# Attention and a two-layer MLP on one core: another order for the first batch and the seam of the layers, with re-timed builds

## The chip, the core and the metric

The kernel runs on one core of a Trainium2 chip. TensorE (PE in the rows) multiplies, VectorE (DVE), ScalarE (ACT) and GpSimd (POOL) do the element-wise work, and SyncE (SP) and ScalarE issue the DMAs. Every engine works through its own instruction stream in order, and waits on semaphores. The metric is the device time of one execution in microseconds, the median of several runs. TensorE's granted clock is 1.00 (2.4 GHz) or 0.50 (1.2 GHz) of full speed at any moment; a row shows the mean over its stretch.

## What is computed

Attention over 4 batches, 8 heads, 576 positions and 64 channels, with a causal window of 128 and a linear bias, and then two feed-forward layers of 512 x 2048 on the 2304 tokens:

```python
rel = pos[:, None] - pos[None, :]
mask = (rel >= 0) & (rel < 128)
scores = np.where(mask, scale * (q @ k.T) - slope * np.abs(rel), -1e9)
attn = np.exp(scores - max); attn = attn / (attn.sum() + 1e-9)
x = (attn @ v)                                  # 2304 tokens x 512
h = x @ w1_in;  x = np.maximum(0.01 * h, h) @ w1_out
h = x @ w2_in;  out = (h / (1 + np.exp(-1.702 * h))) @ w2_out
```

Inputs come as 64-bit floats for the weights and as 32-bit floats for q, k and v. Each 32-bit operand of the two layers is held as a high part and a low part, and a product is three passes (high by high, high by low, low by high).

## The kernel before

**Attention.** The work goes in 32 steps `s`, listed in `steps` (L273): a step is a batch `b`, a group `g` of four heads and a block `i`. For i = 1, 2, 3 it handles two neighbouring 64-row blocks of two head pairs; i = 0 handles the three blocks that are left, with six items for the vector engines in place of four. The function `attention` (L834) emits, for each s, the scores of step s, the products with v of step s - 3 and the transposes of step s - 2 on PE, with the bias and maximum (DVE, L403), the exponentials (ACT, L415), the normalising (POOL, L428), the copies out of PSUM (L442, L489) and the subtraction for the low part (L135) between them. Step s = 0 needs only the first blocks of q and k; i = 2 and 3 need the later blocks too. `load_first` (L340) issues the first loads of q, k, a weight block and v on the SP and ACT queues in the order in which they are written. Eight DMA semaphores go round, so an issue also waits until the eighth DMA ahead of it has landed.

**Weights.** A weight block comes as 64-bit words (`load_w`, 512 KB) and is turned into a high and a low part by `conv_w`: an absolute value and a copy on ACT, five operations on DVE, an addition and a subtraction on POOL, spread over 12 ticks. A tick is a place in the emitted program, three per attention step and one per product group. `wconv` lists the blocks (n, p) in order, p = 0 for the in-weights and p = 1 for the out-weights, `convs` names the steps in which one starts, and `wload` the loads.

**Layer 1.** A round is a chunk `c` of 256 hidden channels and a tile `t` of 384 tokens. `mm1` makes two groups of 12 matmuls per round, `mm2` four groups of 6, and `groups` holds their order. From s = 8 one group runs per attention step as soon as its weights are converted and its tokens are there; the rest run in `layer1` (L738) and at the head of `layer2` (L768).

**Layer 2.** A unit (i, p) multiplies a chunk with a pair of token tiles by seven products (L597, 6 matmuls each) in 13 slots; six of the slots are empty and take an output product `out2` of the unit before (L667, 6 matmuls of 512 columns). The operands x of pair p come from `build_x(p, pace)`: seven copies on ACT (L564) and eleven subtractions on DVE (L135, 128x768), operation d being emitted `int(d * pace)` ticks after the start. The seven hidden results of a unit pass through `gate` (a tanh on ACT, L609, and a multiplication on DVE, L610) and `split` (a copy on ACT, L524, and a subtraction on POOL, L135) before `out2` can use them. `load_out` fetches the out-weights of a unit.

Of the kernel before, what the change touches and what calls it, by code (L numbers as in the profile page):

```python
# [20 lines left out]
CB = 2  # L21
# [10 lines left out]
def attention_mlp_kernel(  # L32
# [24 lines left out]
    def after(d, fn):  # L57
        later.setdefault(step[0] + d, []).append(fn)
# [75 lines left out]
    def sub(e, out, in0, in1):  # L134
        e.tensor_tensor(out=out, in0=in0, in1=in1, op=ALU.subtract)  # L135
# [35 lines left out]
    def conv_w(n, p):  # L171
        early = window[0]
        if early:
            x = 4 * p + n
            af, ops = to_f32(
                n, p, 2, ys[:, 1536:2048].bitcast(U32) if x % 3 == 2 else None,
                ys[:, 2048:2560].bitcast(U32) if x % 2 == 1 else None, (0, 2, 3, 4, 5, 6, 7))
        else:
            af, ops = to_f32(n, p, 4)
        hi, lo = wt[n][:, 2 * p], wt[n][:, 2 * p + 1]  # L180
        run(ops + [
            (10 if early else 7, lambda: nc.scalar.activation(hi, af, AF.Copy)),
            (12 if early else 8, lambda: (
                sub(nc.gpsimd if early else nc.vector, lo, af, hi.bitcast(F32)),
                ready.add((n, p)))),
        ])
# [83 lines left out]

    steps = [(0, g, i) for i in (1, 2, 3, 0) for g in range(2)]  # L273
    steps += [(b, g, i) for b in range(1, B) for g in range(2) for i in (1, 2, 3, 0)]
    NS = len(steps)

# [63 lines left out]
    def load_first(wz):  # L340
        for n in range(2):
            new_qk(n)
        load_q(nc.sync, 0, 0, 0, 4)
        load_q(nc.scalar, 0, 1, 0, 4)
        load_k(0, 0, 4)

        nc.scalar.activation(wz[:, 0:1], wz[:, 1:2], AF.Exp)
        load_k(1, 0, 4)
        load_q(nc.scalar, 1, 0, 0, 4)
        load_q(nc.sync, 1, 1, 0, 4)  # L350
        load_k(0, 4, NKB)
        load_q(nc.sync, 0, 0, 4, NKB)
        load_q(nc.scalar, 0, 1, 4, NKB)
        load_w(*wload.pop())
        load_v_first()
        load_k(1, 4, NKB)
        for a in range(2):
            load_q(nc.sync, 1, a, 4, NKB)
        load_w(*wload.pop())
        load_v(1)  # L360
# [186 lines left out]

    xb = {}  # L550

    def xblocks(extra):
        halves = [xs[:, t, k] for t in (0, 1) for k in range(2)]
# [6 lines left out]
    def build_x(p, pace):  # L560
        b11, b12, b21, b22 = (y1[:, 2 * p + t, 2 * j:2 * j + 2] for j in range(2) for t in range(2))

        def hi(n, src):
            return lambda: nc.scalar.activation(xb[p][n][:, 0], src, AF.Copy)  # L564

        def lo(n, src, e):
            return lambda: sub(e, xb[p][n][:, 1], src, xb[p][n][:, 0].bitcast(F32))

        def diff(out, in0, in1):
            return lambda: sub(nc.vector, out, in0, in1)  # L570


        V = nc.vector
        ops = [
            (0, hi(0, b11)), (1, lo(0, b11, V)), (1, hi(1, b21)), (2, diff(b11, b12, b11)),
            (2, hi(5, b22)), (3, lo(1, b21, V)), (4, lo(5, b22, V)), (5, diff(b12, b22, b12)),
            (6, diff(b22, b22, b11)), (6, hi(3, b12)), (7, hi(2, b22)), (7, lo(2, b22, V)),
            (8, lo(3, b12, V)), (8, hi(4, b11)), (9, diff(b21, b22, b21)), (9, hi(6, b21)),
            (10, lo(4, b11, V)), (11, lo(6, b21, V)),
        ]  # L580
        run([(int(d * pace), fn) for d, fn in ops])
# [9 lines left out]

    def product(i, p, n, out, start, stop):
        w = slots[n]
        x = xb[p][XN[n]]
        ops = [(a, b2, k) for a, b2 in PASS for k in range(2)]
        for m, (a, b2, k) in enumerate(ops):
# [107 lines left out]

    alone = 4
    for j in range(0, alone, 2):
        groups += [(j + c, mm1, f) for c in range(2) for f in range(CB)]
        groups += [(j + c, mm2, e) for c in range(2) for e in range(4)]
    for j in range(alone, NR + 2):
        for ff in range(CB):  # L710
            if j < NR:
# [17 lines left out]
        ch = n // CB - 2  # L729
        return ch < 0 or (pos2 if p else pos1)[0] >= last1[ch] - ahead  # L730

    wconv = [(n, p) for p in range(2) for n in range(2 * CB)]
    wconv += [(n + f, p) for n in range(2 * CB, NF, CB) for p in range(2) for f in range(CB)]
    wload = wconv[:4 * CB]
    wload.reverse()

# [31 lines left out]
    def layer2():  # L768
# [4 lines left out]
        for n in USE:  # L773
            load_in(0, n)

        begun = None
        while groups:
            run_group()
            tick()
            if begun is None and pos2[0] >= NR - 5:  # L780
                begun = step[0]
                build_x(0, 1.5)
        load_out(0)
        assert begun is not None
        after(max(1, begun + 20 - step[0]), lambda: build_x(1, 1.5))
        units = [(c, p) for c in range(NCH) for p in range(2)] + [
            (NCH + c, 2) for c in range(NCH)]
        prev = []
        for k, (i, p) in enumerate(units):
            more = i + 1 < NCH  # L790
            for t, fn in enumerate(unit_ops(i, p)):
# [10 lines left out]
                tick()  # L802
            if p and NCH - 1 <= i < 2 * NCH - 1:
                load_out(i + 1)
            if (i, p) == (NCH - 1, 0):
                after(1, lambda: build_x(2, 1.25))
            prev = [lambda t=t, e=e, i=i, p=p: out2(i, p, t, e) for t in (1, 0) for e in range(3)]
        for _ in range(4):
            tick()
# [19 lines left out]
        for n in range(2 * CB):  # L829
            alloc_w(n)  # L830

    convs = (0, 2, 4, 5, 7, 8, 10, 11)

    def attention():  # L834
        nconv, credit = 0, 0.0
# [124 lines left out]
```

## Time and profile before

| what | value |
|---|---|
| median of 3 runs | 908.07 us (907.67 to 908.46) |
| the profiled execution, its own time | 912.59 us |
| its span | 910.8 us |
| mean granted TensorE clock over the span | 0.982 |
| PE busy | 873.9 us (96%) |
| DVE, ACT, POOL busy | 73%, 47%, 44% |

The span is what the rows cover; 1.79 us of the execution's own time lie around it. The busy share of PE is a mean over stages: the first 80 us, where attention alone runs, differ from the rest, and so do two short stretches near 520 and 765 us. The rows further down are taken from these.

### The profile page before, as it was taken

To read this page: it belongs to the slowest core of one execution; us is meant where nothing else is said; L and a number is where in the kernel's file an instruction comes from. 1 tells how busy PE (TensorE), PEld (TensorE's weight loads), DVE (VectorE), ACT (ScalarE), POOL (GpSimd) and SP (SyncE) were. 2 spreads that over 40 slices of the span, in tenths; PEclk is the share of its full clock that TensorE was granted. 3 is DMA by queue.
4 is the path that set the end of the run, shared out by engine and by line. 5 is a ranking of instruction groups with operands and counts; after the bars stand their busy time and mean duration, and the time that the engine had idled before them with its cause. 6 is when DMAs were issued, how large, how long until landed. Compare 5 with 4: busy or idle time off the path is not lost.

```text
span 910.8 us, 16665 instructions
## 1 busy us (share of the span) xinstructions
PE 873.9 (96%) x6106; PEld 812.6 (89%) x6106; DVE 660.9 (73%) x1337; ACT 427.1 (47%) x1060; POOL 397.9 (44%) x457
## 2 busy tenths in 40 slices
PE   4699999999999999999999989999999998999997
PEld 3577989999999999999999878888888887988896
DVE  4888773688878999899974765777777778344554
ACT  3788885554333444434433455444434344343331
POOL 4697554364445656465662133323333332222221
PEclk7999999999999999999999989999999998999999
DMA  8764432225222342534141242343344327756553
GB/s 211 169 160 105 119 87 72 72 91 170 73 71 70 139 162 70 174 136 162 50 174 70 70 129 100 119 150 110 105 154 153 96 79 200 234 167 207 162 186 70
DMA packets 78626, 116.11 MB, mean 127 GB/s; under 512 B 40912, under 2 KB 41936, under 8 KB 77520
## 3 DMA queue, kind: packets, MB, share of 16 engines
q1 hardware_dynamic: 76784, 114.61, 41.5%
q8 instruction: 49, 0.80, 0.3%
q10 hardware_dynamic: 1760, 0.43, 0.2%
q14 instruction: 33, 0.27, 0.1%
HBM read 87.23 MB, written 27.79 MB: 126 GB/s over the span
## 4 chain that ended last, share of the span: by engine, by line
PE 86%; DVE 5%; issue 3%; DMA 2%; ACT 1%; POOL 1%; SPq 0%; DVEq 0%; POOLq 0%; ACTq 0%
PE mm L667 22%; PE mm L533 11%; PE S L597 10%; PE S L509 10%; PE pt L509 10%; PE O L533 9%; PE pt L597 5%; PE O L597 3%; PE O L469 2%; PE pt L434 2%; PE S L385 2%; PE mm L509 2%; DMA raw<-w1i 1%; DMA y<-v 1%; DVE x L135 1%
## 5 line engine op out<-in xcount | busy, mean ns | idle before, releaser
L135 POOL TENSOR_TENSOR g<-u,g 128x384 fp32r<-128x384 f32 x156 | 171.4, 1103 | 304.8 <-ACT g L524 224.1
L667 PE MATMUL mm<-wB,g 128*128 128x512 f32 x540 | 143.8, 396 | 3.8 <-ACT g L524 2.1
L678 DVE SCALAR_TENSOR_TENSOR y<-mm,y 128x512 f32<-128x512 f32 x126 | 86.9, 689 | 57.8 <-PE mm L667 57.1
L667 PEld LDWEIGHTS mm<-wB,g 128*128 128x128 f32 x540 | 100.8, 189 | 21.8 <-ACT g L524 2.4
L167 POOL TENSOR_TENSOR ca<-ca,cb 128x512 f32<-128x512 f32 x59 | 78.4, 1328 | 52.2 <-DVE cb L165 49.4
L667 PE MATMUL mm<-wB,gm 128*128 128x512 f32 x324 | 87.6, 398 | 3.7 <-POOL gm L135 1.8
L524 ACT ACTIVATE g<-u 128x384 fp32r<-128x384 f32 x156 | 81.3, 522 | 12.8 <-DVE u L610 10.2
L609 ACT ACTIVATE u<-sn 128x384 f32<-128x384 f32 x72 | 37.8, 525 | 91.7 <-DVE sn L625 80.6
L135 POOL TENSOR_TENSOR gm<-u,gm 128x384 fp32r<-128x384 f32 x36 | 36.8, 1036 | 99.0 <-ACT gm L524 65.4
L157 DVE TENSOR_SCALAR ca<-ca 128x512 f32<-128x512 f32 x62 | 46.5, 751 | 45.8 <-ACT ca L156 43.0
L597 PE MATMUL S<-x,wA 128*128 128x384 f32 x384 | 78.9, 341 | 0.0
L597 PEld LDWEIGHTS S<-x,wA 128*128 128x128 f32 x384 | 69.4, 192 | 4.2 <-ACT sn L620 1.3
L667 PEld LDWEIGHTS mm<-wB,gm 128*128 128x128 f32 x324 | 60.5, 190 | 12.6 <-POOL gm L135 2.1
L543 DVE TENSOR_TENSOR y<-y,mm 128x384 f32<-128x384 f32 x88 | 48.2, 548 | 21.2 <-PE mm L533 20.7
L533 PE MATMUL mm<-g,wA 128*128 128x384 f32 x312 | 63.2, 337 | 0.0
L533 PE MATMUL mm<-g,wB 128*128 128x384 f32 x312 | 63.2, 337 | 0.0
L620 ACT ACTIVATE sn<-S 128x384 f32<-128x384 f32 x72 | 34.7, 482 | 55.6 <-PE S L597 55.6
L597 PE MATMUL pt<-x,wA 128*128 128x384 f32 x288 | 58.0, 336 | 0.8 <-DVE sn L625 0.8
L161 DVE SCALAR_TENSOR_TENSOR ca<-raw,ca 128x512 uint32<-128x512 uint32 x62 | 58.5, 944 | 0.2
L165 DVE SCALAR_TENSOR_TENSOR cb<-raw,cb 128x512 f32<-128x512 uint32 x60 | 57.3, 954 | 0.6
L597 PEld LDWEIGHTS pt<-x,wA 128*128 128x128 f32 x288 | 51.4, 188 | 5.4 <-DVE sn L625 1.3
L515 ACT ACTIVATE u<-S 128x384 f32<-128x384 f32 x42 | 20.5, 489 | 74.3 <-PE S L509 69.0
(128 smaller groups left out, 1881.0 us busy)
## 6 DMA issues: line engine op xcount, KB each, us to landing
wA<-w7d SPq DMA_DIRECT2D x112, 256.0 KB, 2.9
w7d<-c SPq DMA_DIRECT2D x8, 1792.0 KB, 6.5
wB<-wod SPq DMA_DIRECT2D x36, 256.0 KB, 4.8
raw<-w1i SPq DMA_DIRECT2D x16, 512.0 KB, 3.7
raw<-w1o SPq DMA_DIRECT2D x16, 512.0 KB, 3.6
raw<-w2o SPq DMA_DIRECT2D x16, 512.0 KB, 4.5
raw<-w2i SPq DMA_DIRECT2D x16, 512.0 KB, 3.5
wod<-wB SPq DMA_DIRECT2D x28, 256.0 KB, 2.9
```

The source lines that it names most:

```text
L135: e.tensor_tensor(out=out, in0=in0, in1=in1, op=ALU.subtract)
L157: lambda: nc.vector.tensor_scalar(af, af, F32_MIN_EXP, F32_MAX_EXP, op0=ALU.max, op1=ALU.min),
L161: lambda: nc.vector.scalar_tensor_tensor(out=a, in0=hi32, scalar=0xC0000000, in1=a, op0=ALU.bitwise_and, op1=ALU.bitwise_or),
L165: lambda: nc.vector.scalar_tensor_tensor(out=bf, in0=lo32, scalar=2.0 ** -52, in1=bf, op0=ALU.mult, op1=ALU.mult),
L167: lambda: nc.gpsimd.tensor_tensor(out=af, in0=af, in1=bf, op=ALU.add),
L509: nc.tensor.matmul(out=h, lhsT=w[:, a, k * 128:(k + 1) * 128], rhs=xs[:, t, b2, k], start=(m == 0), stop=(m == len(ops) - 1),)
L524: nc.scalar.activation(g[:, 0], u, AF.Copy)
L533: nc.tensor.matmul(out=y, lhsT=wt[c * CB + f][:, 2 + a, e * 128:(e + 1) * 128], rhs=gt[r, f][:, b2, :], start=(m == 0), stop=(m == len(ops ...
L543: nc.vector.tensor_tensor(out=acc, in0=acc, in1=y, op=ALU.add)
L597: nc.tensor.matmul(out=out, lhsT=w[:, 256 * a + 128 * k:256 * a + 128 * k + 128], rhs=x[:, b2, k], start=(start and m == 0), stop=(stop an ...
L667: nc.tensor.matmul(out=y, lhsT=gt[i, p, f, t][:, b2, e * 128:(e + 1) * 128], rhs=out_slot(i, f, a), start=(m == 0), stop=(m == len(ops) - 1),)
L678: nc.vector.scalar_tensor_tensor(out=acc, in0=y, scalar=0.5, in1=acc, op0=ALU.mult, op1=ALU.add)
```

## The change

The first batch's steps are written as three of group 0 (i = 1, 2, 3), three of group 1, and then the two with i = 0; they alternated between the groups before. The first loads are put in that order, so the later blocks of q and k of group 0 and the first weight block go ahead of group 1's first blocks. `wconv` now takes both in-blocks of a chunk and then both out-blocks, chunk by chunk, and the eight conversions start in steps 1, 3, 4, 6, 8, 9, 11, 12. In layer 1's first four rounds all groups of chunk 0 on a tile stand ahead of those of chunk 1. The last six groups of layer 1 are left for the six empty slots of layer 2's first unit, the first `load_out` moves behind that unit, and the three builds run at paces 1.8, 1.7 and 1.8 in place of 1.5, 1.5 and 1.25, the second starting 13 ticks after the first (or at once, if these have passed) instead of 20.

```diff
-    steps = [(0, g, i) for i in (1, 2, 3, 0) for g in range(2)]
+    steps = [(0, g, i) for g in range(2) for i in (1, 2, 3)] + [(0, 0, 0), (0, 1, 0)]
...
-        load_k(1, 0, 4)
-        load_q(nc.scalar, 1, 0, 0, 4)
-        load_q(nc.sync, 1, 1, 0, 4)
         load_k(0, 4, NKB)
         load_q(nc.sync, 0, 0, 4, NKB)
         load_q(nc.scalar, 0, 1, 4, NKB)
+        load_q(nc.scalar, 1, 0, 0, 4)
         load_w(*wload.pop())
+        load_k(1, 0, 4)
+        load_q(nc.sync, 1, 1, 0, 4)
...
     for j in range(0, alone, 2):
-        groups += [(j + c, mm1, f) for c in range(2) for f in range(CB)]
-        groups += [(j + c, mm2, e) for c in range(2) for e in range(4)]
+        for c in range(2):
+            groups += [(j + c, mm1, f) for f in range(CB)] + [(j + c, mm2, e) for e in range(4)]
...
-    wconv = [(n, p) for p in range(2) for n in range(2 * CB)]
-    wconv += [(n + f, p) for n in range(2 * CB, NF, CB) for p in range(2) for f in range(CB)]
+    wconv = [(n + f, p) for n in range(0, NF, CB) for p in range(2) for f in range(CB)]
...
-        while groups:
+        while len(groups) > 6:
             run_group()
             tick()
             if begun is None and pos2[0] >= NR - 5:
                 begun = step[0]
-                build_x(0, 1.5)
-        load_out(0)
+                build_x(0, 1.8)
         assert begun is not None
-        after(max(1, begun + 20 - step[0]), lambda: build_x(1, 1.5))
+        after(max(1, begun + 13 - step[0]), lambda: build_x(1, 1.7))
...
-        prev = []
+        prev = [run_group] * len(groups)
...
+            if k == 0:
+                load_out(0)
             if (i, p) == (NCH - 1, 0):
-                after(1, lambda: build_x(2, 1.25))
+                after(1, lambda: build_x(2, 1.8))
...
-    convs = (0, 2, 4, 5, 7, 8, 10, 11)
+    convs = (1, 3, 4, 6, 8, 9, 11, 12)
```

SP's queue at the very start, the two programs against each other (q and k of the first batch, `raw` a weight block, `y<-v` the first v; 256 columns are the first blocks of k, 320 the later ones):

```order
 L297 DMA q<-q 64x4x64 x2
-L303 DMA y<-k 128x2x256 x2
-L297 DMA q<-q 64x4x64 x2
+L303 DMA y<-k 128x2x256
 L303 DMA y<-k 128x2x320
 L297 DMA q<-q 64x5x64 x2
 L127 DMA raw<-w1i 128x1024
+L303 DMA y<-k 128x2x256
+L297 DMA q<-q 64x4x64 x2
 L327 DMA y<-v 128x2x640
 L329 DMA y<-v 64x2x640 x2
```

Group 1's first blocks of k and half of its first q moved behind the first weight block; v and what follows it keep their place.

PE where layer 1 meets layer 2, before (S, O, pt and mm are PSUM tiles; L533 is `mm2`, L597 a product of a unit, L667 `out2`):

```order
L533 MATMUL mm<-g,wB 128x384 x6
L533 MATMUL O<-g,wB 128x384 x6
L597 MATMUL S<-x,wA 128x384 x6
L597 MATMUL O<-x,wA 128x384 x6
L597 MATMUL S<-x,wA 128x384 x6
L597 MATMUL pt<-x,wA 128x384 x6
L597 MATMUL S<-xe,wA 128x384 x12
L597 MATMUL pt<-x,wA 128x384 x6
L597 MATMUL S<-x,wA 128x384 x6
L667 MATMUL mm<-wB,g 128x512 x6
```

and now, from the last group of `layer1`'s order on (the products stand on L599):

```order
L533 MATMUL O<-g,wB 128x384 x6
L599 MATMUL S<-x,wA 128x384 x6
L533 MATMUL mm<-g,wB 128x384 x6
L599 MATMUL O<-x,wA 128x384 x6
L599 MATMUL S<-x,wA 128x384 x6
L533 MATMUL O<-g,wB 128x384 x6
L599 MATMUL pt<-x,wA 128x384 x6
L533 MATMUL mm<-g,wB 128x384 x6
L599 MATMUL S<-xe,wA 128x384 x6
L533 MATMUL O<-g,wB 128x384 x6
L599 MATMUL S<-xe,wA 128x384 x6
L533 MATMUL mm<-g,wB 128x384 x6
```

The first unit's products no longer stand in a row; a group of `mm2` lies in each gap.

DVE from the start of the third build, in unit (7, 1), before (L135 are the build's subtractions, L678 adds up `out2`, L625 and L610 serve the gates):

```order
L135 TENSOR_TENSOR x<-y,x 128x768
L678 SCALAR_TENSOR_TENSOR y<-mm,y 128x512
L135 TENSOR_TENSOR y<-y 128x768
L625 TENSOR_TENSOR sn<-sn,O 128x384
L135 TENSOR_TENSOR x<-y,x 128x768
L610 SCALAR_TENSOR_TENSOR u<-u,sn 128x384
L678 SCALAR_TENSOR_TENSOR y<-mm,y 128x512
L135 TENSOR_TENSOR xe<-y,xe 128x768
L135 TENSOR_TENSOR y<-y 128x768
L678 SCALAR_TENSOR_TENSOR y<-mm,y 128x512
L135 TENSOR_TENSOR y<-y 128x768
L135 TENSOR_TENSOR x<-y,x 128x768
```

and now (L680, L627 and L612 for L678, L625 and L610):

```order
L135 TENSOR_TENSOR x<-y,x 128x768
L680 SCALAR_TENSOR_TENSOR y<-mm,y 128x512
L627 TENSOR_TENSOR sn<-sn,O 128x384
L135 TENSOR_TENSOR y<-y 128x768
L612 SCALAR_TENSOR_TENSOR u<-u,sn 128x384
L680 SCALAR_TENSOR_TENSOR y<-mm,y 128x512
L135 TENSOR_TENSOR x<-y,x 128x768
L680 SCALAR_TENSOR_TENSOR y<-mm,y 128x512
L135 TENSOR_TENSOR xe<-y,xe 128x768
L627 TENSOR_TENSOR sn<-sn,pt 128x384
L680 SCALAR_TENSOR_TENSOR y<-mm,y 128x512
L135 TENSOR_TENSOR y<-y 128x768 x2
```

The subtractions are drawn apart: seven of them stood among these twelve rows, six do now.

## Rows read from the trace of the kernel before

**Rows 1.** The page's head.
```profile
span 910.8 us, 16665 instructions
```

**Rows 2.** Windows: start:end us, length, busy us of each engine, PE clock, DMA.
```profile
42.10:77.50 35.40, 29.28 (x427) 24.50 (x427) 31.38 (x111) 29.61 (x106) 31.43 (x44) 0.95 0.57 142
...
98.10:517.40 419.30, 419.20 (x3078) 414.19 (x3078) 334.85 (x627) 196.90 (x475) 213.64 (x228) 1.00 0.33 108
517.40:534.10 16.70, 11.39 (x44) 9.63 (x44) 14.21 (x18) 8.51 (x16) 5.46 (x4) 0.80 0.09 20
...
763.50:776.30 12.80, 9.15 (x31) 7.77 (x30) 8.68 (x13) 4.12 (x8) 3.67 (x3) 0.73 0.85 226
```

**Rows 3.** Timeline, PE, attention: start us, us, instruction, idle before and releaser.
```profile
21.21 2.15 PE L385 MATMUL mm<-y,q 64*64 64x192 f32 x14 [7.10 <-DMA q<-q]
...
42.08 0.88 PE L385 MATMUL S<-y 64*64 64x192 f32 x16
45.13 1.68 PE L469 MATMUL O<-pt,v 64*64 64x128 f32 x32 [2.17 <-ACT pt L442]
```

**Rows 4.** Chain that ended last, in order of time: start us, us, what.
```profile
16.41 8.29 DMA raw<-w1i
24.72 0.68 ACT ca L156
```

**Rows 5.** Timeline, SP queue, the load of k for batch 1, group 0.
```profile
34.21 0.62 SPq L303 DMA_DIRECT2D y<-k  x1
```

**Rows 6.** The page's DMA issues: count, KB each, median us to landing.
```profile
y<-k SPq DMA_DIRECT2D x6, 576.0 KB, 5.1
```

**Rows 7.** Timeline, PE, where layer 1 meets layer 2.
```profile
516.34 1.21 PE L597 MATMUL pt<-x,wA 128*128 128x384 f32 x6
517.38 1.22 PE L597 MATMUL S<-xe,wA 128*128 128x384 f32 x6
...
525.80 0.50 PE L667 MATMUL mm<-wB,g 128*128 128x512 f32 x1 [2.05 <-ACT g L524]
528.09 2.50 PE L667 MATMUL mm<-wB,g 128*128 128x512 f32 x5 [1.78 <-POOL g L135]
...
534.09 1.55 PE L667 MATMUL mm<-wB,g 128*128 128x512 f32 x6
```

**Rows 8.** Timeline, DVE and POOL, in the same stretch.
```profile
518.96 1.09 POOL L135 TENSOR_TENSOR g<-u,g 128x384 fp32r<-128x384 f32 x1 [10.64 <-ACT g L524]
...
519.11 1.76 DVE L135 TENSOR_TENSOR y<-y 128x768 f32<-128x768 f32 x1
```

**Rows 9.** Timeline, PE, during the third build.
```profile
763.48 1.55 PE L667 MATMUL mm<-wB,g 128*128 128x512 f32 x6
764.87 1.21 PE L597 MATMUL S<-x,wA 128*128 128x384 f32 x6
767.90 0.49 PE L667 MATMUL mm<-wB,gm 128*128 128x512 f32 x1 [1.82 <-ACT gm L524]
770.23 2.50 PE L667 MATMUL mm<-wB,gm 128*128 128x512 f32 x5 [1.84 <-POOL gm L135]
...
776.32 1.54 PE L667 MATMUL mm<-wB,gm 128*128 128x512 f32 x6
```

**Rows 10.** Timeline, DVE and ACT, during the third build.
```profile
764.13 0.54 DVE L610 SCALAR_TENSOR_TENSOR u<-u,S 128x384 f32<-128x384 f32 x1
764.60 0.68 DVE L678 SCALAR_TENSOR_TENSOR y<-mm,y 128x512 f32<-128x512 f32 x1
765.20 0.94 DVE L135 TENSOR_TENSOR y<-y 128x768 f32<-128x768 f32 x1
766.06 0.54 DVE L625 TENSOR_TENSOR sn<-sn,pt 128x384 f32<-128x384 f32 x1
...
766.17 0.84 ACT L564 ACTIVATE x<-y 128x768 fp32r<-128x768 f32 x1 [2.16 <-DVE y L135]
...
766.92 0.92 ACT L524 ACTIVATE gm<-u 128x384 fp32r<-128x384 f32 x2
```

More of the change, by code (lines that the diff above doesn't have):

```diff
@@ L173, in conv_w @@
         if early:
-            x = 4 * p + n
+            x = wconv.index((n, p))
             af, ops = to_f32(
@@ L545, in mm2 @@
         after(1, evac)
-    xb = {}
+    xb, built = {}, set()
     def xblocks(extra):
@@ L566, in lo @@
         def lo(n, src, e):
-            return lambda: sub(e, xb[p][n][:, 1], src, xb[p][n][:, 0].bitcast(F32))
+            return lambda: (sub(e, xb[p][n][:, 1], src, xb[p][n][:, 0].bitcast(F32)),
+                            built.add((p, n)))
         def diff(out, in0, in1):
@@ L593, in product @@
         w = slots[n]
+        assert (p, XN[n]) in built
         x = xb[p][XN[n]]
```

## The prediction

> **What bounds the kernel now.** I first looked at the windows over the whole span. PE never pauses for 419.3 us in the middle [rows 2], and outside three places it is full, so time is PE's own work plus what PE loses at those places: the first 77 us, the seam of the layers (called A, near 520 us) and the third build (B, near 765 us). Anything that PE loses there comes back one for one, since behind each place it is full again and nothing but its own work sets the end.
>
> A: the windows show 11.39 us of work in 16.70, at a clock of 0.80 [rows 2]. In the timeline, neighbouring starts give the undisturbed prices: a product of six 384-column matmuls 1.04 us (516.34 to 517.38, [rows 7]), an `out2` group 1.39 us (763.48 to 764.87, [rows 9]). Between 517.38 and 534.09 stand six products and one `out2`: 6 x 1.04 + 1.39 = 7.63 us. They took 16.71, so A loses **9.08 us**: 16.70 - 11.39 = 5.31 idle, and 3.77 because PE runs slowly after the last two waits (five matmuls in 2.50 us, [rows 7]; 5/6 of 1.39 would be 1.16).
>
> B in the same way: between 763.48 and 776.32 stand two `out2` groups and three products, 2 x 1.39 + 3 x 1.04 = 5.90 us, and 12.84 passed [rows 9]. B loses **6.94 us**, of which 12.80 - 9.15 = 3.65 are idle [rows 2] and the rest is clock.
>
> The start: step 3 waits 7.10 us for its q [rows 3]. From there the steps come every (42.08 - 21.21) / 5 = 4.17 us [rows 3]. Up to 77.5 us no engine is full: PE 29.28, DVE 31.38, ACT 29.61, POOL 31.43 of 35.40 [rows 2]; it is a chain from engine to engine that sets the pace.
>
> **The change, part by part.**
>
> *First steps and loads.* Steps 1 and 2 become those of group 0, whose later q and k now come early; step 3 asks only for group 1's first blocks. The bytes ahead of group 1's last q are the same ones, so that q still lands near 21 to 22 us. The wait stays, but at step 4 instead of 3: **one step more** is behind the kernel when it ends. The chain that follows says whether this is worth something: it goes through the second weight block, landed at 24.72, and ACT's operation on it [rows 4]. That conversion now starts in step 3 instead of 2, so the same block at the same time also stands one step later. Hence one step, 4.17 us. What this collides with: the k of step 8 is issued on SP at 34.21 behind weight loads that wait for conversions [rows 5], none of which gets earlier, and such a load takes 5.1 us [rows 6]: 34.8 + 5.1 = 39.9, where step 8 would like 42.08 - 4.17 = 37.9. PE would wait 2.0 us there; but the next products with v started only at 45.13, after 2.17 us for a copy on ACT [rows 3], and 45.13 - 4.17 = 41.0 is behind 39.9 + 0.9. Only DVE's work of step 8 is late; I charge 0.5, between 0 and 2.
>
> *Order of weights and groups.* From step 8 each step has one group; the first twelve are the same four `mm1` and eight `mm2`, now 2, 4, 2, 4 instead of 4, 8. Two `mm1` leave the stretch up to 77.5 us for the full one after it, where each costs 1.04 more than an `mm2` (12 matmuls against 6): 2.1 us lost. What they free before is one POOL subtraction each (1.09, [rows 8]) and a copy on ACT, on engines at 84 to 89%. I set the balance at -0.4, between -2.5 and +2.
> Start in all: 4.17 - 0.5 - 0.4 = **3.3**, from -0.3 (4.17 - 2 - 2.5) to 6.2.
>
> *Seam A.* The first unit's seven products waited for each other through ACT, DVE and POOL. Six groups of 1.04 us now lie in the gaps. They are moved, not added, so PE's work is unchanged. DVE is the one to check. Prices by neighbouring starts: a build's subtraction 0.86, an addition or gate 0.47, an `out2` sum 0.60 [rows 10]; I price an `mm2` sum as a gate, 0.47. Before, seven products (7.3 us of PE) covered eight subtractions and six small operations, 6.9 + 2.8 = 9.7 us: DVE had to fall behind by 2.4 us, and with POOL's interference by more. Now 13 slots x 1.04 = 13.5 us cover ten subtractions (the second build starts in the first unit's first tick), six sums and six small ones, 8.6 + 2.8 + 2.8 = 14.2 us: nearly level. Two waits should remain. The second product into S waits for ACT's snapshot, behind two build copies (0.84 each, [rows 10]) of which the first waits for a DVE difference: about 0.7. And the first `out2` comes 4 x 1.04 = 4.2 us after the product whose gate it uses, where a later unit has 2 x 1.04 + 2 x 1.39 = 4.9. The chain needs two tanh and two copies on ACT (about 0.9 a pair, as the pair in [rows 10]), two gates on DVE (0.9) and two subtractions on POOL (2.1, [rows 8]), 4.8 of which about 1.0 overlaps; a build's copy (0.84) and DVE's lag where three operations fall in one tick (about 1.3) stand ahead: 5.9 in all, so a wait of about 1.8. Left over 2.5; gain 9.1 - 2.5 = **6.6**, up to 9.1 if both waits close, down to 9.1 - 2.5 - 3.8 = 2.8 if the clock drops as before. `load_out` behind the unit costs nothing: SP reaches it early, and what it overwrites is last read by layer 1's last `mm1`, 13 or more groups ahead of its use.
>
> *Third build B.* At pace 1.25 all eleven subtractions fall in one unit: 11 x 0.86 + 6 x 0.60 + 7 x 0.47 = 16.4 us of DVE beside 7 x 1.04 + 6 x 1.39 = 15.6 us of PE. ACT shows the result: a build copy waits 2.16 us for DVE, and the gates' two copies stand behind it at 766.92 [rows 10]; PE waits for just these [rows 9]. At 1.8 seven of the eleven fall there: 16.4 - 4 x 0.86 = 13.0 of 15.6, and the four others in the next unit, 3.4 + 6.9 = 10.3 of 15.6. The lag goes. The latest block is read one tick or more after its emission, so the slower pace itself adds at most a wait of one subtraction, 0.9; I take 0.2. Gain **6.7**, between 4 and 6.9.
>
> Sum: 3.3 + 6.6 + 6.7 = 16.6 us. The profiled execution took 912.59 (span 910.8, [rows 1]), so 896.0 under the profiler. The median of the runs is 4.5 lower than that execution; the losses are waits and clock in the program itself, so I take them off the median whole: 908.07 - 16.6 = 891.5.
>
> **A rule beside the rows.** A subtraction of the build on DVE took 1.76 us from 519.11 and ended 0.82 after POOL's subtraction had ended at 520.05, as if it had started only then [rows 8]; it is the longest of six among the 33 that ran for 1.3 us or more. The Trainium skill, page "SBUF — State Buffer", section "Who interferes with whom", has a rule that agrees and speaks against packing builds and gates together: a DVE instruction with two SBUF inputs and a GpSimd instruction that reads SBUF exclude each other, and whoever comes first keeps the shared ports for the whole instruction. Taken alone, it would hold four subtractions of the first unit by 0.82 each, 3.3 us more than the 14.2 of DVE, and with these on PE's path the sum would be 13.3 and the time 894.8; my sum has one such meeting in the lag of 1.3.
>
> **The rivals.**
> *Clock at A.* The waits left at A drop the clock again, as it did after 525.80 [rows 7]: gain 2.8 there, 12.8 in all, 895.3. For it: DVE is only level. Against: 2.5 us of waiting are left of 5.3.
> *The start gives nothing.* The k of step 8 and the two moved `mm1` eat the step: start -0.3, 13.0 in all, 895.1. For it: SP's order. Against: 45.13.
> *It doesn't do what it says at B*: ACT's queue and not the pace set the wait, and B keeps its loss: 9.9 in all, 898.2. Against: ACT waited for DVE.
> *Slower.* The builds run beside more gates and sums, and every subtraction meets POOL: 33 x (1.76 - 0.94) = 27.1 us more of DVE [rows 8, 10], all of it shown to PE where DVE is level. It decides above (16.6 + 1.8) / 0.82 = 23 stretched subtractions of 33, and ends at 908.07 - 16.6 + 27.1 = 918.6. Against: six were stretched, and each POOL subtraction can hold one of them only; a unit has four. By the Trainium skill's rule above it is this lock that would decide.
>
> **How the numbers follow.** Forecast 0.72 (gains of 13 to 22), clock at A 0.12, no gain at the start 0.09, B kept 0.03, slower 0.03, and 0.01 for a sum that cancels. The terms' ends make 908.07 - (6.2 + 9.1 + 6.9) = 885.9 and 908.07 - (-0.3 + 2.8 + 4.0) = 901.6; the range 885.5 to 900 leaves out the corner where all three are at their worst. Faster by over 0.2% (1.8 us, about what a measurement of this kernel can tell from no change) 0.96, within 0.01, slower 0.03.
>
> **What would show it.** Right: PE's longest DMA wait stands before step 4 and not 3, and step 8's scores start at 38 to 41 us; in the first unit of layer 2 PE's waits sum to under 3 us at a clock of 1.00; no wait and no lower clock in the third build, with DVE below nine tenths there; PE full otherwise. Wrong: a wait of several us for k at step 8 or for a weight at steps 8 to 16; gates' copies behind build copies on ACT at A; a product of the last pair waiting for its x; build subtractions near 1.7 us in a row.

## The result and the profile after

The changed kernel takes **896.47 us**, median of 4 runs (896.23 to 896.67), where the kernel before took 908.27 in the same comparison (907.67 to 908.75, 4 runs): ratio 0.987, 95% interval 0.9853 to 0.9887. That is 11.8 us less. The forecast was 891.5 in a range of 885.5 to 900: the sign and the range held, the forecast itself was 5 us too low.

The head of the page after, against [rows 1]:

```profile
span 894.4 us, 16658 instructions
...
PE 865.6 (97%) x6106; PEld 807.3 (90%) x6106; DVE 653.5 (73%) x1337; ACT 428.5 (48%) x1060; POOL 406.6 (45%) x457
```

Windows of after (start:end us, length, busy us of each engine, PE clock, DMA), against [rows 2]: attention from the scores of step 10 to those of step 16, the full middle, the seam A from the first product of layer 2 to the second unit's second `out2`, and the third build B.

```profile
48.30:79.68 31.38, 26.23 (x421) 22.44 (x421) 28.30 (x101) 25.54 (x95) 27.65 (x39) 0.95 0.48 126
98.10:502.20 404.10, 404.00 (x2949) 399.42 (x2939) 322.47 (x598) 188.78 (x452) 210.43 (x220) 1.00 0.33 110
502.26:523.67 21.41, 18.73 (x103) 17.68 (x103) 21.36 (x31) 12.57 (x22) 7.70 (x5) 1.00 0.08 23
749.60:763.40 13.80, 13.80 (x70) 12.39 (x69) 11.86 (x18) 7.96 (x14) 3.42 (x4) 1.00 0.80 220
```

B is full at a clock of 1.00. The middle still never pauses. At A PE is idle for 2.68 us in place of 5.31, and DVE is now busy all the time there, 21.36 of 21.41 us.

The stretch of [rows 9], from the last `out2` that reads `g` to the second that reads `gm`, takes 5.91 us now, where it took 12.84:

```profile
753.51 1.55 PE L669 MATMUL mm<-wB,g 128*128 128x512 f32 x6
...
759.42 1.55 PE L669 MATMUL mm<-wB,gm 128*128 128x512 f32 x6
```

PE's timeline of after in the attention part (start us, us, instruction, idle before and what ended it), against [rows 3]; the scores of steps 3, 4, 8 and 10, the first product with v, and the first `mm2`:

```profile
13.08 0.88 PE L385 MATMUL mm<-y,q 64*64 64x192 f32 x16
15.86 0.62 PE L469 MATMUL O<-pt,y 64*64 64x128 f32 x10 [1.90 <-DMA y<-v]
...
19.83 1.23 PE L385 MATMUL S<-y,q 64*64 64x192 f32 x16
...
36.75 0.88 PE L385 MATMUL S<-y 64*64 64x192 f32 x16 [0.99 <-DMA y<-k]
...
48.30 0.88 PE L385 MATMUL S<-y 64*64 64x192 f32 x16
...
53.79 0.44 PE L533 MATMUL mm<-g,wA 128*128 128x384 f32 x1 [2.41 <-POOL g L135]
```

Step 3 no longer waits for its q, and neither does step 4; the longest wait for a load is now the 1.90 us for the first v. Step 8 stands 5.33 us earlier than in [rows 3], step 10 7.15 (55.45 before); part of that is a late load in the trace of before, as the next section shows. A wait is new: the first `mm2` directly follows the `mm1` whose result it reads, and waits 2.41 us for POOL.

PE at A in after, against [rows 7], and POOL and DVE in the same stretch, against the 1.09 of [rows 8]:

```profile
517.36 0.50 PE L669 MATMUL mm<-wB,g 128*128 128x512 f32 x1
520.33 1.42 PE L669 MATMUL mm<-wB,g 128*128 128x512 f32 x5 [2.47 <-POOL g L135]
521.59 1.21 PE L599 MATMUL O<-x,wA 128*128 128x384 f32 x6
522.63 1.20 PE L599 MATMUL S<-x,wA 128*128 128x384 f32 x6
```

```profile
510.30 2.44 POOL L135 TENSOR_TENSOR g<-u,g 128x384 fp32r<-128x384 f32 x1 [7.66 <-ACT g L524]
516.97 3.30 POOL L135 TENSOR_TENSOR g<-u,g 128x384 fp32r<-128x384 f32 x2 [4.24 <-ACT g L524]
```

```profile
510.04 1.82 DVE L135 TENSOR_TENSOR x<-y,x 128x768 fp32r<-128x768 f32 x2
...
512.24 1.31 DVE L135 TENSOR_TENSOR y<-y 128x768 f32<-128x768 f32 x1
```

Of the four waits at A one long one is left, 2.47 us at the first `out2`, and PE ran on at full clock behind it; another of 0.21 stands at 514.08. POOL's subtractions for the gates take 2.44 us, and 3.30 for two (two at the same place took 2.67 before, at 525.36).

### The profile page after: what moved, and what is told of

It reads as the page before. It is cut to its first block, busy times and chain, and to the rows that moved or that the text cites. A ratio compares the mean times of both kernels' runs of the same rounds, so it can differ in the third digit from the quotient of the medians.

```text
span 894.4 us, 16658 instructions
## 1 busy us (share of the span) xinstructions
PE 865.6 (97%) x6106; PEld 807.3 (90%) x6106; DVE 653.5 (73%) x1337; ACT 428.5 (48%) x1060; POOL 406.6 (45%) x457
## 4 chain that ended last, share of the span: by engine, by line
PE 87%; DVE 4%; issue 2%; DMA 2%; POOL 2%; ACT 1%; SPq 0%; ACTq 0%; DVEq 0%; POOLq 0%
PE mm L669 21%; PE mm L533 11%; PE S L599 10%; PE pt L509 10%; PE O L533 10%; PE S L509 10%; PE pt L599 5%; PE O L599 2%; PE O L469 2%; PE pt L434 2%; PE mm L509 2%; PE S L385 2%; DMA q<-q 1%; DMA y<-v 1%; POOL g L135 1%
## 5 line engine op out<-in xcount | busy, mean ns | idle before, releaser
L135 POOL TENSOR_TENSOR g<-u,g 128x384 fp32r<-128x384 f32 x156 | 177.1, 1140 | 298.2 <-ACT g L524 217.8
L680 DVE SCALAR_TENSOR_TENSOR y<-mm,y 128x512 f32<-128x512 f32 x126 | 86.9, 690 | 61.7 <-PE mm L669 61.2
L135 POOL TENSOR_TENSOR gm<-u,gm 128x384 fp32r<-128x384 f32 x36 | 38.4, 1081 | 95.1 <-ACT gm L524 76.1
L599 PE MATMUL S<-x,wA 128*128 128x384 f32 x384 | 77.3, 336 | 0.6 <-ACT sn L622 0.6
L599 PEld LDWEIGHTS S<-x,wA 128*128 128x128 f32 x384 | 67.9, 188 | 4.8 <-ACT sn L622 1.5
L533 PE MATMUL mm<-g,wA 128*128 128x384 f32 x312 | 63.6, 337 | 2.4 <-POOL g L135 2.4
L533 PE MATMUL mm<-g,wB 128*128 128x384 f32 x312 | 63.3, 337 | 0.0
L599 PE MATMUL pt<-x,wA 128*128 128x384 f32 x288 | 58.0, 335 | 0.2 <-DVE sn L627 0.2
L533 PEld LDWEIGHTS mm<-g,wA 128*128 128x128 f32 x312 | 54.5, 188 | 2.7 <-POOL g L135 2.7
L599 PEld LDWEIGHTS pt<-x,wA 128*128 128x128 f32 x288 | 51.4, 188 | 4.7 <-DVE sn L627 0.5
```

Source lines behind the costliest of these rows:

```text
L533: nc.tensor.matmul(out=y, lhsT=wt[c * CB + f][:, 2 + a, e * 128:(e + 1) * 128], rhs=gt[r, f][:, b2, :], start=(m == 0), stop=(m == len(ops ...
L599: nc.tensor.matmul(out=out, lhsT=w[:, 256 * a + 128 * k:256 * a + 128 * k + 128], rhs=x[:, b2, k], start=(start and m == 0), stop=(stop an ...
L680: nc.vector.scalar_tensor_tensor(out=acc, in0=y, scalar=0.5, in1=acc, op0=ALU.mult, op1=ALU.add)
```

## Experiments

Between the two profiled executions lie 16.4 us (910.8 and 894.4), as the forecast said (16.6), and between the medians 11.8. So the first question was what the profiled execution of before, 4.5 us above its own median, had lost more than others, and the second what each part of the change gives alone.

### The kernel before once more

> The kernel before, unchanged, for another profile and more times. Theory 1: the first profiled execution was 4.5 us above its own median because PE lost more than usual at A and B (longer waits there and a longer time at the low clock). Then a new profiled execution near 908 us shows A (517.38 to 534.09 in the first trace, 16.71 us, 9.08 lost) and B (763.48 to 776.32, 12.84 us, 6.94 lost) with a sum of losses near 11.5 us in place of 16.0, and the attention part as it was. Theory 2: the 4.5 us lie outside A and B, so a profile near 908 us has A and B with 16 us lost again and is shorter elsewhere, and the parts of the change give less together than one by one.

Median 910.67 (908.68 to 912.66, 12 runs), the other runs of before in this comparison 910.29 (908.28 to 913.15, 19 runs). One execution of this kernel is thus a draw from some 5 us. The new profile (span 908.9) shows A and B as in [rows 7, 9]: the same four waits, 20.99 us from the first product to the second unit's second `out2` (20.87 in the first trace). **Theory 1 falls.** The difference lies at the start: here step 3 begins at 19.44 (21.21 in [rows 3]) and step 20 at 95.54 (98.08).

PE's timeline of this execution at step 3:

```profile
19.44 1.84 PE L385 MATMUL mm<-y,q 64*64 64x192 f32 x16 [6.70 <-DMA q<-q]
20.77 1.80 PE L469 MATMUL O<-pt,y 64*64 64x128 f32 x32
22.50 1.12 PE L434 MATMUL pt<-ident,st 128*128 128x128 f32 x6
23.54 0.72 PE L385 MATMUL S<-y,q 64*64 64x192 f32 x12
```

The first loads land at different times from execution to execution. In the five executions with the old start this wait was 7.10, 6.70, 5.01, 4.76 and 6.85 us, and step 20 began at 98.08, 95.54, 95.86, 95.96 and 97.34 (the last of these lost 1.0 us between steps 10 and 16, and not at the loads).

### The three parts alone

The start alone (steps, loads, `wconv`, `convs`, `groups` as in the diff ahead of the prediction, nothing else):

> Only the order of the first steps, the loads, the weight conversions and the groups of chunk 0 and 1; seam and builds as before. Both theories: the start gains 4.73 us in the traces (from 98.08 to 93.35 at the scores of step 20), and nothing at A or B depends on it, so 908.1 - 4.7 = 903.4 us. A rival of mine from the prediction (the start gives nothing): 908.

908.59 us (906.08 to 910.0), ratio 0.9977 (0.9962 to 0.9991): 2.1 us by the ratio, with 0.8 and 3.5 as the ends. The 4.73 read from the first two traces was too much, since half of it was the late q of one execution.

The seam alone:

```diff
-        while groups:
+        while len(groups) > 6:
...
-                build_x(0, 1.5)
-        load_out(0)
+                build_x(0, 1.8)
...
-        after(max(1, begun + 20 - step[0]), lambda: build_x(1, 1.5))
+        after(max(1, begun + 13 - step[0]), lambda: build_x(1, 1.7))
...
-        prev = []
+        prev = [run_group] * len(groups)
...
+            if k == 0:
+                load_out(0)
```

> Only the seam of the layers: the last six groups of layer 1 fill the empty slots of the first unit, paces 1.8 and 1.7, second build after 13 ticks, the first out-weights loaded behind the unit; start and third build as before. Theory 1: the seam gains 5.7 us against the profiled execution, but less against the timed runs: 1.5 to 4 us, 904 to 906.5. Theory 2: 5.7 us, 902.4.

906.13 us (904.38 to 907.61), ratio 0.9949 (0.9934 to 0.9964): 4.6 us, with 3.3 and 6.0 as the ends, between the two theories.

The third build alone:

```diff
-                after(1, lambda: build_x(2, 1.25))
+                after(1, lambda: build_x(2, 1.8))
```

> Only the third build at pace 1.8 in place of 1.25. Theory 1: 6.5 us against the profiled execution, less against the timed runs: 3 to 5 us, 903 to 905, so that start, seam and third build alone sum to the 11.8 us of the whole change. Theory 2: 6.5 us, 901.5, and the three sum to 16 to 17, more than the whole.

904.02 us (903.83 to 905.07), ratio 0.9928 (0.9915 to 0.9942): 6.5 us, as theory 2 had it. PE's waits of this kernel from 700 us to the end (total us, times, longest) are a single one:

```profile
PE S L597 <- DVE xe L135: 0.2, 1, 0.2
```

The three sum to 13.2 us, each within about 1.4. The whole change on another chip:

> The changed kernel itself beside the kernel before on this chip. By the traces so far, before in its second profile against after: the start 2.2 us (95.54 to 93.35 at step 20's scores), the seam 4.7 (step 20's scores to the fourth output product of the second unit, 443.44 to 438.51, less the clock), the third build and the rest 7: 14 in all, so 896 to 897 where before takes 910.3. If the ratio of 0.987 holds here too, 898.5, and the three parts overlap somewhere.

897.96 us (896.79 to 899.51) against 909.73 (908.22 to 911.33), ratio 0.9873 (0.9857 to 0.989): 11.6 us, with 10.0 and 13.0 as the ends. The intervals of the sum and of the whole overlap; that the parts take something from each other is not shown.

The traces show where. In us: the start of the scores of steps 10 and 20, the time between steps 10 and 16, from step 20 to the second unit's fifth `out2` (A's end; the expectation above counts it as the fourth, without the divided first), and from there to the `out2` of [rows 9] at 776.32 (B's end):

| kernel | step 10 | 10 to 16 | step 20 | 20 to A's end | A's end to B's end |
|---|---|---|---|---|---|
| before, first trace | 55.45 | 29.23 | 98.08 | 443.31 | 234.93 |
| before again | 52.92 | 29.22 | 95.54 | 443.44 | 235.16 |
| third build alone | 53.32 | 29.24 | 95.96 | 443.11 | 228.34 |
| seam alone | 53.17 | 29.29 | 95.86 | 439.76 | 234.07 |
| start alone | 49.27 | 31.11 | 94.04 | 443.11 | 233.99 |
| after | 48.30 | 31.38 | 93.35 | 438.51 | 227.56 |
| full change again | 48.18 | 31.34 | 93.19 | 439.25 | 227.92 |
| paces without fillers (next section) | 53.70 | 30.24 | 97.34 | 442.13 | 233.97 |

The means that follow are of the first seven rows. The B column falls by 6.6 (means of the old and the new pace, 234.54 and 227.94). The A column falls by 4.1 (443.24 to 439.17), and after's first execution was the best of the three. At step 10 the new start is 4.6 us ahead (means 53.14 and 48.58, the late first row left out), gives 2.0 of it back by step 16 (29.25 and 31.28), and is 2.3 ahead at step 20 (95.79 and 93.53). These means sum to 2.3 + 4.1 + 6.6 = 13.0 us. The six steps are not the same in every execution: one with the old start, the last row, took 30.24 us for them, and the other executions of the new start, with its copies as they are, 31.04 to 31.72.

### Fillers or paces at the seam

The kernel before with the paces and the 13 ticks of the seam, without the fillers:

```diff
-                build_x(0, 1.5)
+                build_x(0, 1.8)
...
-        after(max(1, begun + 20 - step[0]), lambda: build_x(1, 1.5))
+        after(max(1, begun + 13 - step[0]), lambda: build_x(1, 1.7))
```

> The kernel before with the two builds of the seam at paces 1.8 and 1.7 (13 ticks) and no fillers in the first unit. Theory: the gain at the seam comes from the six mm2 groups in the gaps; without them more subtractions fall in a first unit that has only seven products as cover, so the four waits there stay or grow: 0 to 3 us slower than before. Rival: the paces bring a part of the 4.6 us of the seam alone.

909.09 us (907.62 to 912.09) against 909.4, ratio 0.9995 (0.9985 to 1.0005): no change. PE's first `out2` in its timeline waits twice as before, only in other shares:

```profile
523.95 0.51 PE L667 MATMUL mm<-wB,g 128*128 128x512 f32 x1 [0.93 <-ACT g L524]
526.65 2.13 PE L667 MATMUL mm<-wB,g 128*128 128x512 f32 x5 [2.19 <-POOL g L135]
```

So the paces alone bring no gain that can be measured in the median (the ends are -0.5 and 1.4 us; in the trace A is 1.1 us shorter, 442.13 against 443.24 in the mean), and the seam needs the six groups in the gaps. The groups with the old paces were not run, so whether the paces add something to them is not shown.

### Why the start gives 2 us back

The changed kernel with the old order of weights and groups, and the changed kernel without a group in step 10:

```diff
-        for c in range(2):
-            groups += [(j + c, mm1, f) for f in range(CB)] + [(j + c, mm2, e) for e in range(4)]
+        groups += [(j + c, mm1, f) for c in range(2) for f in range(CB)]
+        groups += [(j + c, mm2, e) for c in range(2) for e in range(4)]
...
-    wconv = [(n + f, p) for n in range(0, NF, CB) for p in range(2) for f in range(CB)]
+    wconv = [(n, p) for p in range(2) for n in range(2 * CB)]
+    wconv += [(n + f, p) for n in range(2 * CB, NF, CB) for p in range(2) for f in range(CB)]
```

> The changed kernel with the old order of weights and groups (both chunks' in-weights and mm1 first), new steps, loads and conversion times. Theory 3: the step gained at the start (3.7 to 4.0 us at step 10's scores) is spent between steps 10 and 20 (45.05 us in after against 42.62 in before) by the mm2 that directly follows its mm1 (2.41 us of waiting for POOL) and the slow clock behind it. Then steps 10 to 20 take 43 to 43.7 and the kernel is 0.5 to 1.5 us faster than the full change (one group is moved to the full stretch, 1.04 us). Theory 4: the eight conversions, which end one step later in both, set the end of the start, whatever the groups: within 0.5 us of the full change, or slower by the group moved.

```diff
-            credit += 1
+            credit += int(s != 10)
```

> The changed kernel with no group in step 10, so that the first mm2 runs one step later. Theory 3: the wait of 2.41 us and the slow clock behind it go, one group of 1.04 us moves to the full stretch: 0.5 to 1.5 us faster than the full change. Theory 4: 0 to 1 us slower.

With the old groups 897.91 us (897.06 to 898.84), ratio 0.9868 (0.9855 to 0.9881), the same as the full change beside it, though no `mm2` waits for POOL at the start any more: steps 10 to 16 take 31.04 us, against 31.34, and steps 10 to 20 44.71, where theory 3 wanted 43 to 43.7. Without the group in step 10, 901.05 (899.13 to 902.55), 3.1 slower. **Theory 3 falls**: the wait of 2.41 us is idle time that PE has anyway. Without the group, PE waits about as long for DVE at the next scores:

```profile
53.48 1.74 PE L385 MATMUL S<-y 64*64 64x64 f32 x24 [2.56 <-DVE sm L403]
```

From step 16 on PE is full, and there the skipped slot costs: step 16 begins at 80.25 against 79.52, step 20 at 95.54 against 93.19, the first product of layer 2 at 505.79 against 502.12. An `mm1` of 2.08 us left the free stretch for the full one, and a group of 1.04 the steps ahead of step 20.

The next suspect is DVE. Windows up to step 10 and from 10 to 16, of before again and of the full change (DVE is the third engine):

```profile
0.00:52.92 52.92, 35.61 (x498) 27.67 (x498) 38.91 (x159) 34.52 (x128) 34.31 (x65) 0.90 0.75 187
52.92:82.14 29.22, 25.26 (x422) 21.45 (x421) 25.23 (x98) 25.04 (x92) 26.18 (x40) 1.00 0.61 128
```

```profile
0.00:48.18 48.18, 38.67 (x499) 29.38 (x499) 35.94 (x156) 35.01 (x128) 33.11 (x63) 0.82 0.87 207
48.18:79.52 31.34, 26.21 (x421) 22.19 (x420) 28.03 (x101) 25.41 (x95) 27.66 (x39) 0.95 0.48 126
```

DVE does 64.1 us up to step 16 in one (38.91 + 25.23) and 64.0 in the other (35.94 + 28.03). Ahead of step 10 the changed kernel starts its conversions in steps 1, 3, 4, 6, 8 and 9, the kernel before in 0, 2, 4, 5, 7 and 8, and each is spread over 12 ticks (a step has four of them in the listing, and a group one more; the text on the kernel before says three). Of the conversions' operations on DVE, 28 ran ahead of step 10 in the kernel before and 23 in the changed one: 3.0 us of DVE's work are left behind (38.91 - 35.94), and DVE works them off between steps 10 and 16, where it is busy for 28.03 of 31.34 us. POOL is nearly as busy there, 27.66 us.

To test it, the second copy of the transposes in steps 13 to 16 went from DVE to ACT:

```diff
-                att_evac(s - 2, 1, nc.scalar if s < 13 else nc.vector)
+                att_evac(s - 2, 1, nc.scalar if s < 17 else nc.vector)
```

> The changed kernel with the second copy of the transposes in steps 13 to 16 on ACT in place of DVE: four copies of about 0.5 us leave DVE. Theory 4 (DVE, busy 28.03 of 31.34 us between the scores of steps 10 and 16, sets how long these six steps take): 1 to 2 us less there and in the kernel. Rival: the chain from engine to engine sets it, or ACT (25.41 of 31.34) becomes late: no change or slower by up to 1.

896.32 us (894.78 to 898.88) against 909.4, ratio 0.9855 (0.9839 to 0.9871). The window from step 10 to 16:

```profile
48.86:78.59 29.73, 25.49 (x422) 22.10 (x421) 25.56 (x98) 25.76 (x95) 27.98 (x39) 0.94 0.50 132
```

DVE has 2.47 us less to do and the six steps take 1.61 us less, while POOL does as much as before in the shorter time (27.98 of 29.73), so POOL does not set it. DVE is not full either, 25.56 of 29.73: whether its sum of work or its place in the chain from engine to engine holds the steps, this run does not separate. The medians of this kernel and of the full change differ by as much (1.64), but they are from two comparisons, and their intervals overlap. The same edit also stands in a pair within one comparison (below), with 1.9, and there the six steps take 29.75 us in place of 31.44. By its ratio this was the fastest of all kernels run.

### What is left at the seam

The changed kernel with the first build earlier and the second later:

```diff
-                build_x(0, 1.8)
+                build_x(0, 1.5)
...
-        after(max(1, begun + 13 - step[0]), lambda: build_x(1, 1.7))
+        after(max(1, begun + 19 - step[0]), lambda: build_x(1, 1.25))
```

> The changed kernel with the first build at pace 1.5 and the second 19 ticks after it at pace 1.25, in place of 1.8, and 13 ticks at 1.7: fewer of the builds' subtractions in the first unit of layer 2, where nine start now (503.69 to 514.26) and DVE is busy all the time, and more of them ahead of it and behind it, where it is not. Theory 5: the wait of 2.47 us for POOL at the first out2 comes from DVE: POOL's subtractions for the gates take 2.44 and 3.30 for two there in place of 1.0 each, since DVE's subtractions stand in their way, and DVE's own gates are late. Then the wait falls below 1.5 us, POOL's subtractions are shorter, and the kernel is 1 to 3 us faster than the full change (897.96 with before at 909.73: ratio 0.984 to 0.986). Rival: the distance from the first gates to the first out2 is too short whatever DVE does: wait 2 us or more, same as the full change (0.987).

899.96 us (899.14 to 902.46), ratio 0.9898 (0.9883 to 0.9912): slower than the full change by 2 us, where 1 to 3 us faster was expected. (With the edit of the copies on both sides, in one comparison, it is 1.7: 898.06 below against 896.32.) Yet a part of the expected mechanism is there. POOL and PE in the timeline of this kernel:

```profile
516.62 2.72 POOL L135 TENSOR_TENSOR g<-u,g 128x384 fp32r<-128x384 f32 x2 [6.18 <-ACT g L524]
...
519.39 1.43 PE L669 MATMUL mm<-wB,g 128*128 128x512 f32 x5 [1.70 <-POOL g L135]
...
531.88 1.35 PE L599 MATMUL S<-x,wA 128*128 128x384 f32 x6 [2.70 <-ACT sn L622]
```

The wait at the first `out2` fell from 2.47 to 1.70, not below the 1.5 expected, and POOL's two subtractions from 3.30 to 2.72, near the 2.67 of the kernel before. But a wait of 2.70 us stands in the next unit instead, where after had 0.61 and the full change again none. ACT and POOL just ahead of it:

```profile
529.52 1.26 POOL L167 TENSOR_TENSOR ca<-ca,cb 128x512 f32<-128x512 f32 x1
...
530.82 0.63 ACT L217 ACTIVATE wB<-ca 128x512 fp32r<-128x512 f32 x1 [1.85 <-POOL ca L167]
531.35 0.47 ACT L622 ACTIVATE sn<-S 128x384 f32<-128x384 f32 x1
```

A conversion of out-weights and the later build's subtractions share DVE in that unit. A gate among them ran at 527.38 on DVE, where after has it at 525.39, so POOL's subtraction for it (528.56, 1.00 us) came just ahead of the conversion's addition and not well before it. The addition ended at 530.78, and the snapshot of S stands in ACT's queue behind the copy that waits for it: it starts at 531.35 (530.17 in after), while PE comes to this place 0.91 us earlier than in after. DVE's work was moved from one place where PE feels it to another.

The two edits together:

> The two edits together on the changed kernel: later builds, and the copies of steps 13 to 16 on ACT. They lie 400 us apart with PE full between them, so the gains add: 2 to 5 us faster than the full change if both theories hold.

898.06 us (897.52 to 899.39), ratio 0.9874 (0.9862 to 0.9887): 1.9 less than the later builds alone, on the same chip and in the same comparison. The gain at the start and the loss at the seam add. Against the full change (0.9873) nothing is gained, since the later builds bring a loss; 2 to 5 us were expected.

One more run had every output product one slot later, with seven groups of layer 1 left over:

```diff
-        while len(groups) > 6:
+        while len(groups) > 7:
...
-            prev = [lambda t=t, e=e, i=i, p=p: out2(i, p, t, e) for t in (1, 0) for e in range(3)]
+            prev = prev + [lambda t=t, e=e, i=i, p=p: out2(i, p, t, e) for t in (1, 0) for e in range(3)]
```

> The changed kernel with seven groups of layer 1 left over for the units instead of six, so that every output product runs one slot (1.04 us or more) later. If the first out2's wait for POOL at the seam (2.47 us at 520.33) is only a matter of the distance from the gate, it falls to 1.4 or less there and the kernel gains 1 to 2.5 us on the full change. If DVE, full there (5.00 of 5.00 in 510 to 520), sets the pace of the first unit, the wait stays or moves to the next product: no gain.

937.47 us, ratio 1.031. In this kernel the last output product of a unit reads the out-weights of the next one, so it computes something else, and PE waits for their loads (total us, times, longest):

```profile
PE mm L669 <- DMA wB<-wod: 23.9, 15, 5.1
```

At the first `out2` there is no wait in it, so the distance from the gates counts; but two products ahead of it now wait 0.79 us for DVE and 0.64 for ACT, and one behind it 3.12 for ACT. As a whole it says nothing on the time of the full change.

## Why the prediction was right, and where it was wrong

**What bounds the kernel** held: the long middle stayed as it was. From step 20 to the first product of layer 2 pass 415.14 us before, and 408.93 + 6 x 1.04 = 415.17 in the full change, with its six groups moved.

**The start** came to 3.3 in the forecast, 2.1 in the runs of the start alone and 2.3 in the means of the traces. Two terms of it were wrong and cancelled in part. The step gained was priced 4.17 - 0.5 = 3.7; step 10 came 4.6 us earlier. The wait for group 1's q did not move to step 4: that step starts at 19.83 without a wait for a load. The 21 to 22 us for this q came from one late execution; in the four others with the old start it was there by 19.4 to 20.0. For the same reason step 8, at 36.75, came ahead of the 38 to 41 that were named as a sign. The k of step 8 cost PE 0.99 us in after, nothing in the full change again and 2.34 with the old groups, where the text saw a wait of 2.0 and charged 0.5.

The balance of -0.4 for the moved groups should have been -2.3, and by another mechanism: not the `mm1`, whose place makes no difference that can be measured, but the work of the conversions that DVE had left when step 10 came earlier. (That DVE's work holds steps 10 to 16 is shown by the moved copies; no run moved the conversions alone, so their share is argued from the windows.) "The same block at the same time also stands one step later" saw the block's landing and not the DVE work behind it. [rows 2] showed DVE at 31.38 of 35.40 up to 77.5 us; that was the place to ask what the steps that come earlier would have to carry.

**Seam A** is the term that was mis-sized most: 6.6 forecast, 4.1 in the traces, 4.6 for the seam alone. The total of the waits in the first unit was right (2.68 in place of the 2.5), their places were not: 2.47 stand at the first `out2`, where 1.8 were expected, and a second product into S that waits for ACT's snapshot comes only in the next unit (0.61 in after, up to 0.33 in the five below).

What failed is the step from waits to time: the 2.5 us of waiting were taken for all that is left over. From the first product of layer 2 to the second unit's second `out2` stand ten products, six groups and one `out2`, 16 x 1.04 + 1.39 = 18.03 us. After took 21.41, so it lost 3.38: 2.68 idle, and 0.70 in matmuls that ran longer around the two stops. Five other executions with the fillers (the seam alone, the full change again, the old groups, the skipped group, the copies moved to ACT) took 22.96 to 22.99 and lost 4.9 to 5.0: with the same wait of 2.46 or 2.47 us, but with a granted clock of 0.82 or 0.83 over some ten us around and behind it, where after had 1.00. That is the rival that was given 0.12 (gain 2.8). DVE, called nearly level with 14.2 us of work for 13.5, was busy for 21.36 of 21.41 us, and POOL's two subtractions for the first `out2` took 3.30 us in place of the 2.1 priced. PE in the full change again:

```profile
520.18 1.50 PE L667 MATMUL mm<-wB,g 128*128 128x512 f32 x5 [2.47 <-POOL g L135]
521.48 2.12 PE L597 MATMUL O<-x,wA 128*128 128x384 f32 x6
523.40 1.87 PE L597 MATMUL S<-x,wA 128*128 128x384 f32 x6
```

Against after's 1.21 and 1.20 for the same two products. From 520.18 to the next `out2` at 525.11 are 4.93 us, in after 3.34.

**Third build B** was right in mechanism and size: 6.7 forecast, 6.5 alone, 6.6 in the traces. DVE took 11.86 of 13.80 us there, below the nine tenths named, and the one wait left is 0.2, as charged; it stands behind the window.

**The sum** of the terms is 13.0 by the traces, not 16.6: 2.5 of the difference are A, 1.0 the start. The medians show 11.6 to 11.8; the intervals of the two ratios reach to 13.0 and 13.4. Of the last 1.2 us, 0.4 are lost behind B's end, where the columns stop: from there to the end of the span pass 134.85 us in the mean of the eight traces with the new third build and 134.41 in the five with the old, and the wait of 0.2 lies there. The rest is allowed by the spread of the runs, but not explained. **The base** was taken rightly: the losses at A and B are in every trace of the old seam and the old third build, so they come off the median. That the two profiled executions lay 16.4 us apart, almost the forecast's 16.6, was chance: before's q was 2.3 us late (98.08 against 95.79 at step 20), and after's clock at A stayed up. Read against each other, these two traces alone would have confirmed a sum that was too large.

**Of the rivals**, the one at the start (k and two `mm1` eat the step) came half true, by way of DVE, and the clock at A came nearest: it gave 895.3. The slower one did not come: of the build's 33 subtractions on DVE six took 1.3 us or more, as many as before, and the longest again 1.76. What grew is the other side, POOL's subtractions at A.

## What to carry to other kernels

A step that comes earlier gains only what the engines behind it let through: count the work of the fullest of them up to the point where the bound engine is full again, before and after, and not the place of a label. A wait that is left over costs more than its length where the clock falls behind it. One profiled execution is a draw; where the whole time spreads over 5 us, look in which part that execution differs before its terms are taken off a median. Work that is moved off a crowded unit lands in the next one, and a copy that waits there holds whatever stands behind it in its engine's queue.

## What was not expected of the hardware

With DVE's subtractions in a row, a POOL subtraction of 128x384 took 2.44 us and two took 3.30, with fewer of them ahead two took 2.72, where one took 1.00 in the next unit of that kernel (at 528.56) and 1.09 in [rows 8]. The Trainium skill, page "SBUF — State Buffer", section "Who interferes with whom", has that a DVE instruction with two SBUF inputs and a GpSimd instruction that reads SBUF contend for ports that are locked for one of them. The rows agree, with either side held: POOL's subtraction of 510.30 began while DVE did two of its own and ended at 512.74, 0.88 us after these; DVE's next one, from 512.24, ended at 513.55, 0.81 after POOL's.

The granted clock behind the same stop is not the same each time. After 2.46 or 2.47 us of idle time for POOL at the first `out2`, PE stayed at full speed in one of six executions and fell to half speed for part of the next products in the other five (1.21 us against 2.12 in the two traces shown, 1.82 and 1.20 for the two products with the old groups). The work on PE ahead of the stop is the same; what decides it stayed open. In the two kernels with the later builds it stayed at full speed behind 1.70 and 1.69 us of idle time, and fell behind 2.70 and 2.72 (0.83 in some ten us around each).

The first loads of one start do not land at the same time in every execution: the wait for q at step 3 ended with step 3 starting at 21.21, 19.44, 19.75, 19.62 and 20.02 us in five executions with the same order of loads, and step 4 at 25.88, 23.54, 24.33, 24.32 and 24.83: 1.8 and 2.3 us between the first and the last.
